# First softmax of taps ahead of the weights' loads, the last four tokens in twos, and a new order of steps

## The chip, the core and the metric

One NeuronCore of a Trainium2 chip runs the kernel. Its engines are TensorE (PE, with PEld for its weight loads), VectorE (DVE), ScalarE (ACT), GpSimd (POOL) and SyncE (SP, which issues DMAs); ACT issues a few DMAs too. The metric is the device time of one execution in microseconds (us); lower is better.

## The reference

`x` is 8 x 4160 x 192 and `weight_gen` 8 x 4160 x 8 x 7, both float32. Each token mixes itself and the six tokens before it, with seven taps per head; what comes out goes through a two-layer block of 192 -> 1024 -> 192.

```python
w = exp(weight_gen - max); w = w / (sum(w) + 1e-9)        # over the 7 taps of a head
x = einsum('bshk,bskhg->bshg', w, windows of x)           # causal, 8 heads of 24 columns
h = x @ w_in                                              # 1024 columns
solu = h * softmax(h)
ln = (solu - mean) / sqrt(var + 1e-6) * g_ln
out = ln @ w_out
```

## The kernel before

The 33,280 tokens lie on 128 partitions, 260 in a row on each, so a "token" below is one step of 128 rows; there are 260. They come in chunks of 4, 8, 8 and then 16 tokens (`starts` = 0, 4, 12, 20, 36, ...). For a chunk the kernel loads `xt` and `wt` and does the softmax of the taps in seven steps, t0 to t6: maximum on DVE (L112), subtraction on POOL (L114), exponential on ACT (L118), sum on DVE (L120), a copy on ACT (L122), reciprocal on DVE (L124), product on POOL (L126). ACT sums the squares of `xt` (L145).

POOL then does attention for a group of four tokens (two in the first four): a product over seven taps (L174) and two additions (L180, L182), which leave `half`. DVE adds its two parts into `a` (fin, L433). From there a token, or a pair, goes: a copy on ACT (dup, L439); transposition on PE (xT, L450); high part on ACT (xhi, L458); low part on DVE (xld, L479); first product on PE (mm1, L491 and L494); maximum on DVE (max, L505); exponential on ACT (exp, L509); product with it on DVE (solu, L515); squares on ACT (sq, L521); high half of the result on ACT (hi, L528); low half on DVE (lo, L532); a transposing DMA by SP (tr, L540); second product on PE (mm2, L580); scaling on ACT (out, L591); and for four tokens a store by SP (od, L594). The scales of a group of tokens are six short steps, f0 to f5, in turn on ACT (L555, L559/L561, L567) and DVE (L552). A first product writes `h` into one of three PSUM buffers, so that of token t waits for sq and lo of token t-3; second products share one buffer `po`, except for the odd two of the last four tokens, which take a buffer of `h`.

Before the first product the weights are converted: `w_in` in three parts (`raw_a` twice, and `raw_b`, shown as `hl`), `w_out` in four parts c0 to c3, each in three DVE instructions (L241, L244, L246), two on ACT (L248, L249) and three more on DVE (L253, L256, L260). Copies, remainders and norms follow (wa_hi, wa_lo, wb_hi, wb_lo, L284).

Each engine runs its own instructions in the order in which they were written. The order of the preparation stands in the code; that of all later steps comes from `issue_order`, a planner: it goes through a table of steps with an engine, an assumed cost, the steps waited for and sometimes an assumed earliest time (`ready`), and gives each free engine the able step with the lowest key, which is the token's number plus the step's number in `URGENCY`. `free` says when each engine is thought to come out of the preparation.

Of the kernel before, what the change touches and what calls it, by code (L numbers as in the profile page):

```python
# [26 lines left out]
def tile_kernel(ctx: ExitStack, tc: tile.TileContext, x, weight_gen, w_in, w_out, g_ln, out):  # L27
# [9 lines left out]
    RUN = B * S // P  # L37
    PB = P // B
    TG = 4
# [27 lines left out]
    def load_x(c, part=0):  # L67
        t0, n = starts[c], starts[c + 1] - starts[c]
        if part == 0:
            xs[c] = io.tile([P, (TC + HALO) * D], F32, name="xt")  # L70
        xt = xs[c]
        xv = xt.rearrange("p (t d) -> p t d", d=D)
        if c == 0:

            nc.gpsimd.memset(xt[:, : HALO * D], 0.0)
            nc.sync.dma_start(xv[:, HALO : HALO + n, :], x_run[:, :n, :])
            for b in range(B):
                queue = nc.sync if b % 2 else nc.scalar
                queue.dma_start(
                    xv[b * PB + 1 : (b + 1) * PB, :HALO, :],  # L80
                    x_run[b * PB : (b + 1) * PB - 1, RUN - HALO :, :],
                )
        elif t0 < HALO:
            first = xs[0].rearrange("p (t d) -> p t d", d=D)
            nc.sync.dma_start(xv[:, HALO : HALO + n, :], x_run[:, t0 : t0 + n, :])
            nc.sync.dma_start(xv[:, :HALO, :], first[:, t0 : t0 + HALO, :])
        else:
            cuts = [(HALO + n) * k // LOADS for k in range(LOADS + 1)]
            r0, r1 = cuts[part], cuts[part + 1]
            nc.sync.dma_start(xv[:, r0:r1, :], x_run[:, t0 - HALO + r0 : t0 - HALO + r1, :])  # L90
# [9 lines left out]
    TAP_STEPS = 7  # L100

    def softmax_taps(c, step):
        n = (starts[c + 1] - starts[c]) * H
        w3 = ws[c][:, : n * K].rearrange("p (n k) -> p n k", k=K)
        if step == 0:
            m = small.tile([P, TC * H], F32, name="wm", bufs=2)[:, :n]
            y = small.tile([P, TC * H], F32, name="wy", bufs=2)[:, :n]
            taps[c] = m, y
        m, y = taps[c]
        wide = [P, n, K]  # L110
        if step == 0:
            nc.vector.tensor_reduce(m, w3, axis=AX.X, op=ALU.max)  # L112
        elif step == 1:
            nc.gpsimd.tensor_tensor(  # L114
                out=w3, in0=w3, in1=m.unsqueeze(2).broadcast_to(wide), op=ALU.subtract
            )
        elif step == 2:
            nc.scalar.activation(w3, w3, AF.Exp)  # L118
        elif step == 3:
            nc.vector.tensor_reduce(m, w3, axis=AX.X, op=ALU.add)  # L120
        elif step == 4:
            nc.scalar.activation(y, m, AF.Copy, bias=1e-9)  # L122
        elif step == 5:
            nc.vector.reciprocal(y, y)  # L124
        elif step == 6:
            nc.gpsimd.tensor_tensor(  # L126
                out=w3, in0=w3, in1=y.unsqueeze(2).broadcast_to(wide), op=ALU.mult
            )
# [59 lines left out]
    w_in = w_in.bitcast(I32)  # L188
    w_out = w_out.bitcast(I32)
    load_x(0)  # L190
    raw_a = att.tile([P, 2 * FF], I32, name="raw_a", bufs=1)

    raw_b = big.tile([P, FF], I32, name="hl", bufs=3)
# [29 lines left out]
    column = const.tile([P, 1], F32, name="column")  # L223
    minus = const.tile([P, P], F32R, name="minus")
    nc.vector.tensor_scalar_mul(minus, ident, -1.0)

    for step in range(TAP_STEPS):
        softmax_taps(0, step)

    scratch = {}  # L230

# [173 lines left out]

    def stat_group(t):

        n = 2 if t < 2 * TG else TG
        return n if t % n == n - 1 else 0


    def group(t):

        if t < TG:
            return 2 if t % 2 == 0 else 0
        return TG if t % TG == 0 else 0

# [225 lines left out]


URGENCY = dict(
    a00=3.1, a01=2.3, a02=-28.9, a03=-6.5, a04=-3.6, a10=80, a11=-25.4, a12=-13, a13=-10, a14=10.4,
    attA=85.1, attB=2.4, b0=120.9, b1=-144.6, b2=138.3, b3=-1.5, b4=54.3, c00=-28.1, c01=85.1,
    c02=6.8, c10=-25.3, c11=31.3, c12=-72.7, c20=99.4, c21=-5.6, c22=10.2, c30=-149.7, c31=-14.5,
    c32=-100.3, dup=52.6, exp=-129.5, f0=8.2, f1=-120.4, f2=-71.5, f3=-118.4, f4=-66.1, f5=-45.6,
    fin=18.4, hi=-11, lo=33, lw=18.7, lx0=10.2, lx1=-115.4, lx2=-109.1, lx3=-20.7, max=-30,  # L650
    mm1=25.5, mm2=0.4, n0=-7.5, n1=11.8, n2=-1.8, n3=-113.6, n4=-8.6, n5=-69, n6=-123.6, od=-6.9,
    out=-81.2, p30=22.9, p31=0.5, p4=9.7, p5=12.6, p6=11.6, p70=-10.2, p71=-8.7, p80=20.3, p81=5.9,
    q00=7.1, q01=-5.1, q02=118.9, q10=-15.7, q11=20.7, q12=16.8, q20=100.6, q21=-95.2, q22=20.4,
    q30=143.8, q31=81.5, q32=98.3, solu=-7.6, sq=5, t0=5.1, t1=-3.7, t2=77.9, t3=44.1, t4=-26.5,
    t5=110.1, t6=267.2, tr=-13, v00=170.9, v01=5.1, v02=44, v03=0.2, v1=54.2, v2=58.8, v3=-12.2,
    v4=1, v5=21.2, xT=-66.9, xhi=-46.7, xld=30,
)


def issue_order(run, starts, group, stat_group, loads):  # L660
# [5 lines left out]

    PE, DVE, ACT, SP, POOL = range(5)
    SAME, CROSS = (25, 127, 143, 0, 102), 130
    free = [3000, 5900, 5000, 12000, 9050]
    steps, number = [], {}  # L670

    def add(name, t, engine, cost, *after, ready=0):
# [3 lines left out]
    def once(name, engine, cost, *after, ready=0):  # L676
        add(name, 0, engine, cost, *((x, 0) for x in after), ready=ready)
# [2 lines left out]
    parts = ["a0", "b", "a1", *(f"c{f}" for f in range(4))]  # L680
    for n, part in enumerate(parts):
        w_in, size = n < 3, 512 if n < 3 else 384
        at = (9000, 10500, 12000)[n] if w_in else 15000
        before = () if w_in else (f"{parts[n - 3]}4", "n" + {"a0": "0", "a1": "1", "b": "2"}[parts[n - 3]]) if n < 6 else ("q00",)
        if n:
            before += (parts[n - 1] + "0",)
        once(part + "0", DVE, 3 * (60 + size), *before, ready=at)
        once(part + "1", ACT, 2 * (190 + 0.85 * size), part + "0")
        once(part + "2", DVE, 3 * (60 + 1.04 * size), part + "1")
        if w_in:  # L690
            once(part + "3", ACT, 190 + 0.75 * size, part + "2")
            once(part + "4", DVE, 60 + 1.04 * size, part + "3")
            once("n" + {"a0": "0", "a1": "1", "b": "2"}[part], DVE, 60 + 1.04 * size, part + "2")
        else:
            f = n - 3
            once(f"q{f}0", ACT, 700, part + "2")
            once(f"q{f}1", PE, 660, f"q{f}0", *([f"q{f - 1}1"] if f else ["n6"]))
            once(f"q{f}2", ACT, 520, f"q{f}0")
    add("p30", 0, DVE, 868, ("q31", 0), ("mm1", 1))
# [31 lines left out]
        add("v4", t, DVE, 80, ("v3", t))  # L731
        add("v5", t, ACT, 240, ("v4", t))

    add("v00", 0, ACT, 1800, ready=9000)
    add_norms(0, 0)
    for c in range(1, len(starts) - 1):
        t, before = starts[c], starts[c - 1] if c > 1 else -1
        short = starts[c + 1] - t < 16
        if c > 1:
            add("lw", t, SP, 1270, last_group(c - 3))  # L740
            add("lx0", t, SP, 1540, last_group(c - 2), *parts_of(c - 2))
            for n in range(1, loads):
                add(f"lx{n}", t, SP, 1540, (f"lx{n - 1}", t))
        whole = starts[c + 1] - t == 16
        for part in range(4 if whole else 1):
            size = 830 if whole else 1800
            if c > 1:

                load = min(part + 1, loads - 1) if whole else loads - 1
                add(f"v0{part}", t, ACT, size, (f"lx{load}", t))  # L750
            else:
                add(f"v0{part}", t, ACT, size, ready=15000)
        add_norms(c, t)
        n = (starts[c + 1] - t) * 8
        on = (DVE, POOL, ACT, DVE, ACT, DVE, POOL)
        wide = 60 + 7.3 * n
        costs = (wide, 13.5 * n, 100 + 6 * n, wide, 100 + n, 60 + 6.3 * n, 13.5 * n)
        for k in range(7):
            if k:
                add(f"t{k}", t, on[k], costs[k], (f"t{k - 1}", t))  # L760
            elif c > 1:
                add("t0", t, on[k], costs[k], ("lw", t), ("t6", before))
            else:
                add("t0", t, on[k], costs[k], ready=12000)
# [4 lines left out]
    for i, t in enumerate(groups):  # L769
        c, full = chunk_of(t), group(t) == 4  # L770
        after = [("attB", groups[i - 1])] if i else []
        if c:
            after.append(("t6", starts[c]))
        if c > 1:
            after.append((f"lx{loads - 1}", starts[c]))
        add("attA", t, POOL, 14990 if full else 7500, *after, ready=15000 if c == 1 else 9000)
        add("attB", t, POOL, 3510 if full else 1800, ("attA", t), ("fin", groups[i - 2] if i > 1 else -1))
        old = t // 4 * 4 - 12
        add("dup", t, ACT, 307 if full else 200, ("fin", t))
        add("fin", t, DVE, 1710 if full else 880, ("attB", t), ("xT", old + 2 if old >= 0 else -1))  # L780
# [144 lines left out]
```

## Time and profile before

| | us |
|---|---|
| median of 3 runs (lowest, highest) | 1347.44 (1345.54, 1348.4) |
| profiled execution: its own time | 1347.67 |
| its span | 1345.8 |
| busy: PE, POOL, DVE, ACT | 1246.8, 1247.7, 1210.2, 1162.8 |

The span runs from the first to the last recorded instruction; 1.87 us of the profiled execution's time lie outside it. A row of the timeline reads: start, duration, engine, line, operation, out<-in and their shapes, and in brackets the idle time before it and what ended that. A row of a table of stretches gives the busy time of each engine in it, with the number of its instructions. "issue" is time in which an engine waited for nothing that the profile shows.

### The profile page before, as it was taken

What the parts mean: (1) busy time and instruction counts of PE and PEld (TensorE: products, weight loads), DVE (VectorE), ACT (ScalarE), POOL (GpSimd) and SP (SyncE); (2) the same over time, 40 slices, a digit from 0 to 9 for tenths busy, and PEclk for the clock granted to TensorE, in tenths of its full rate; (3) what the DMA queues carried; (4) which work ended last, traced back from release to release, by engine and by line L of the source; (5) the groups of instructions that cost most, each with busy time, mean ns of one, the idle gap of its engine ahead of it and who ended that gap; (6) DMA issues with size and microseconds to landing.
All of it is one profiled execution on the core that took longest, in us unless ns stands there. A gap on an engine that the chain in (4) does not pass through costs nothing.

```text
span 1345.8 us, 25810 instructions
## 1 busy us (share of the span) xinstructions
PE 1246.8 (93%) x9900; PEld 970.8 (72%) x9900; DVE 1210.2 (90%) x1588; ACT 1162.8 (86%) x2318; POOL 1247.7 (93%) x241
## 2 busy tenths in 40 slices
PE   0588899999999999999999999999999999999997
PEld 0365677777777777777777777777777777777776
DVE  5988899999999999999999999999999999889994
ACT  3778889889898988989898998989898898988886
POOL 5989899999999999999999999999999999999930
PEclk9899999999999999999999999999999999999999
DMA  5277668797886889688797968878787877976776
GB/s 180 74 159 169 139 134 201 123 207 137 155 179 134 196 137 208 125 179 163 129 202 140 191 140 180 162 128 203 140 193 137 183 150 138 183 134 123 133 134 130
DMA packets 565307, 210.31 MB, mean 156 GB/s; under 512 B 544456, under 2 KB 545864, under 8 KB 565184
## 3 DMA queue, kind: packets, MB, share of 16 engines
q1 hardware_dynamic: 563208, 206.55, 75.7%
q10 hardware_dynamic: 1976, 2.12, 0.6%
q8 instruction: 78, 1.28, 0.4%
q14 instruction: 45, 0.37, 0.1%
HBM read 46.15 MB, written 25.56 MB: 53 GB/s over the span
## 4 chain that ended last, share of the span: by engine, by line
ACT 43%; DVE 35%; issue 11%; PE 7%; DMA 2%; POOL 1%; SPq 0%; ACTq 0%; POOLq 0%
ACT hl L528 12%; ACT e L521 12%; DVE h L515 11%; DVE hl L532 11%; ACT e L509 9%; DVE stats L505 5%; DVE a L433 4%; ACT junk L145 3%; PE po L580 3%; PE h L494 2%; ACT x_hi L458 2%; ACT ot L591 2%; DMA hlT<-hl 2%; PE h L491 1%; DVE x_lo L479 1%
## 5 line engine op out<-in xcount | busy, mean ns | idle before, releaser
L174 POOL TENSOR_TENSOR pr<-xt,wt 128x5376 f32<-128x5376 f32 (+1 forms) x66 | 631.6, 9569 | 2.7
L580 PE MATMUL po<-w_hl,hlT 128*128 128x192 f16 x6192 | 555.1, 246 | 17.3 <-ACT ot L591 12.6
L580 PEld LDWEIGHTS <-hlT 128*128 128x128 f16 x6240 | 505.9, 98 | 83.2 <-issue 75.5
L515 DVE SCALAR_TENSOR_TENSOR h<-h,row,e 128x1024 f32<-128x1024 f32 x260 | 333.8, 1285 | 19.1 <-ACT e L509 16.9
L528 ACT ACTIVATE hl<-h 128x1024 f16<-128x1024 f32 x260 | 266.0, 1029 | 98.4 <-DVE h L515 55.4
L532 DVE SCALAR_TENSOR_TENSOR hl<-h,hl 128x1024 f16<-128x1024 f32 x260 | 316.5, 1218 | 36.8 <-ACT e L521 34.4
L180 POOL TENSOR_TENSOR pr<-pr 128x2304 f32<-128x2304 f32 (+1 forms) x66 | 333.0, 5045 | 5.2
L505 DVE TENSOR_REDUCE stats<-h 128x1 f32<-128x1024 f32 x260 | 316.3, 1217 | 3.9 <-PE h L494 3.3
L509 ACT ACTIVATE e<-h,stats 128x1024 f32<-128x1024 f32 x260 | 293.3, 1128 | 16.1 <-DVE stats L505 15.5
L521 ACT ACTIVATE e<-h,stats 128x1024 f32<-128x1024 f32 x260 | 293.0, 1127 | 1.1 <-DVE hl L532 1.0
L494 PE MATMUL h<-wa_hi,x_hi 128*128 128x512 f32 x520 | 234.0, 450 | 0.0
L182 POOL TENSOR_TENSOR half<-pr 128x1536 f32<-128x1536 f32 (+1 forms) x66 | 225.8, 3421 | 5.2
L494 PE MATMUL h<-wa_lo,x_hi 128*128 128x512 f32 x520 | 206.4, 397 | 0.0
L494 PE MATMUL h<-wa_hi,x_lo 128*128 128x512 f32 x520 | 205.9, 396 | 0.0
L494 PEld LDWEIGHTS h<-wa_hi,x_hi 128*128 128x128 f32 x520 | 98.1, 189 | 107.1 <-issue 95.5
L491 PE MATMUL h<-wb_hi,x_hi 64*128 64x512 f32 x520 | 131.0, 499 | 17.1 <-DVE hl L532 11.2
L433 DVE TENSOR_REDUCE a<-half 128x768 f32<-128x1536 f32 (+1 forms) x66 | 117.2, 1776 | 0.0
L591 ACT ACTIVATE ot<-po,stats 128x192 f32<-128x192 f32 x258 | 112.4, 436 | 3.6 <-PE po L580 3.6
L494 PEld LDWEIGHTS h<-wa_hi,x_lo 128*128 128x128 f32 x520 | 98.4, 189 | 23.2
L494 PEld LDWEIGHTS h<-wa_lo,x_hi 128*128 128x128 f32 x520 | 99.0, 190 | 12.0
L491 PE MATMUL h<-wb_hi,x_lo 64*128 64x512 f32 x520 | 104.2, 395 | 0.0
L450 PE MATMUL pa<-ident,a 128*128 128x128 f32 x520 | 81.2, 278 | 23.9 <-DVE x_lo L479 13.2
(89 smaller groups left out, 1072.0 us busy)
## 6 DMA issues: line engine op xcount, KB each, us to landing
out_dram<-ot SPq DMA_DIRECT2D x65, 384.0 KB, 3.3
xt<-in_x_dram SPq DMA_DIRECT2D x30, 576.0 KB, 4.8
xt<-in_x_dram SPq DMA_DIRECT2D x30, 480.0 KB, 4.4
wt<-in_weight_gen_dram SPq DMA_DIRECT2D x15, 448.0 KB, 4.8
hlT<-hl SPq DMA_TRANSPOSE x260, 4.7
xt<-in_x_dram SPq DMA_DIRECT2D x3, 384.0 KB, 4.6
raw_a<-in_moe_w_in_dram ACTq DMA_DIRECT2D x2, 512.0 KB, 7.4
raw<-in_moe_w_out_dram ACTq DMA_DIRECT2D x1, 768.0 KB, 12.2
```

Of the source, the lines that this page charges most:

```text
L174: nc.gpsimd.tensor_tensor(out=window(pr, 0, [(TG * D, K), (HG, n * H), (1, HG)]), in0=window(xt, t * D, [(D, K), (HG, n * H), (1, HG)]), i ...
L180: nc.gpsimd.tensor_tensor(out=pr[:, :3], in0=pr[:, :3], in1=pr[:, 3:6], op=ALU.add)
L182: nc.gpsimd.tensor_tensor(out=half, in0=window(pr, 0, [(2 * TG * D, 2), (D, n), (1, D)]), in1=window(pr, TG * D, [(5 * TG * D, 2), (D, n), ...
L491: nc.tensor.matmul(h[:, fs], lhs[rows, 1, :], rhs[rows], start=n == 0, stop=False)
L494: nc.tensor.matmul(h[:, fs], lhs[:, 0, :], rhs[:, fs], start=False, stop=n == 2)
L505: nc.vector.tensor_reduce(stat(t, NMAX), h_of[t], axis=AX.X, op=ALU.max, negate=True)
L509: nc.scalar.activation(e, h_of[t], AF.Exp, bias=stat(t, NMAX), accum_out=stat(t, Z))
L515: nc.vector.scalar_tensor_tensor(out=h, in0=h, scalar=row(t, SCALE), in1=e, op0=ALU.mult, op1=ALU.mult, accum_out=stat(t, M))
L521: nc.scalar.activation(e_of.pop(t), h_of[t], AF.Square, bias=stat(t, M), scale=-float(FF), accum_out=stat(t, Q),)
L528: nc.scalar.activation(hl[:, 0, :], h_of[t], AF.Copy, scale=2.0**14)
L532: nc.vector.scalar_tensor_tensor(out=hl[:, 1, :], in0=h_of[t], scalar=2.0**14, in1=hl[:, 0, :], op0=ALU.mult, op1=ALU.subtract,)
L580: nc.tensor.matmul(po[:, :D], hlT[:, half * NJ + j, :], w2_hl[:, j, w, :], start=n == 0, stop=n == len(terms) - 1,)
```

## The change

It has three parts. The seven softmax steps of the first chunk are written right after the loads of its `wt` and `xt`, ahead of the loads of the weights. The last four tokens go through attention in two groups of two (`group`), and their scales are computed in two groups of two (`stat_group`). And the order is made anew: all 100 numbers of `URGENCY`, three numbers of `free` and several `ready` times are others, and `q{f}0`, which scales a part of `w_out`, now waits for two steps of the conversion of `w_in` too.

```diff
     load_x(0)
+    for step in range(TAP_STEPS):
+        softmax_taps(0, step)
     raw_a = att.tile([P, 2 * FF], I32, name="raw_a", bufs=1)
...
     nc.vector.tensor_scalar_mul(minus, ident, -1.0)
-
-    for step in range(TAP_STEPS):
-        softmax_taps(0, step)
...
     def stat_group(t):
-        n = 2 if t < 2 * TG else TG
+        n = 2 if t < 2 * TG or t >= RUN - TG else TG
...
     def group(t):
-        if t < TG:
+        if t < TG or t >= RUN - TG:
             return 2 if t % 2 == 0 else 0
...
-    a00=3.1, a01=2.3, a02=-28.9, a03=-6.5, a04=-3.6, a10=80, a11=-25.4, a12=-13, a13=-10, a14=10.4,
+    a00=116.4, a01=5.1, a02=-29.3, a03=20.5, a04=44.5, a10=8.5, a11=-82.2, a12=-38.6, a13=-3.9,
...
-    free = [3000, 5900, 5000, 12000, 9050]
+    free = [3000, 5600, 7700, 12000, 6200]
...
-        at = (9000, 10500, 12000)[n] if w_in else 15000
+        at = (12000, 12000, 12500)[n] if w_in else 20000
...
-            once(f"q{f}0", ACT, 700, part + "2")
+            once(f"q{f}0", ACT, 700, part + "2", "a02", "a12")
...
-    add("v00", 0, ACT, 1800, ready=9000)
+    add("v00", 0, ACT, 1800, ready=10000)
...
-                add(f"v0{part}", t, ACT, size, ready=15000)
+                add(f"v0{part}", t, ACT, size, ready=21500)
...
-        add("attA", t, POOL, 14990 if full else 7500, *after, ready=15000 if c == 1 else 9000)
+        add("attA", t, POOL, 14990 if full else 7500, *after, ready=21500 if c == 1 else 10000)
```

The changed kernel is one line shorter, so most lines of the program stand one number lower there.

What this does to the order shows at three places. The first is DVE at the start. `wm` and `wy` are the taps' maxima, sums and reciprocals, 32 columns for the first chunk and 64 for the second; `minus` is a constant; `h<-raw_a` and `h<-hl` are the conversion of `w_in`. Before:

```order
L112 TENSOR_REDUCE wm<-wt 128x32
L225 TENSOR_SCALAR minus<-ident 128x128
L241 TENSOR_SCALAR h<-raw_a 128x512
L244 TENSOR_SCALAR h<-raw_a 128x512
L246 TENSOR_SCALAR h<-h 128x512
L241 TENSOR_SCALAR h<-hl 128x512
L244 TENSOR_SCALAR h<-hl 128x512
L120 TENSOR_REDUCE wm<-wt 128x32
L246 TENSOR_SCALAR h<-h 128x512
L124 RECIPROCAL wy<-wy 128x32
```

And DVE at the same place now:

```order
L112 TENSOR_REDUCE wm<-wt 128x32
L227 TENSOR_SCALAR minus<-ident 128x128
L120 TENSOR_REDUCE wm<-wt 128x32
L124 RECIPROCAL wy<-wy 128x32
L151 TENSOR_REDUCE row<-squares_x 128x1
L112 TENSOR_REDUCE wm<-wt 128x64
L240 TENSOR_SCALAR h<-raw_a 128x512
L243 TENSOR_SCALAR h<-raw_a 128x512
L245 TENSOR_SCALAR h<-h 128x512
L240 TENSOR_SCALAR h<-hl 128x512
```

The sum and the reciprocal of the first chunk's taps moved ahead of the conversion, and so did a sum of squares and the maximum of the second chunk's taps, which before stood eleven rows behind the first instruction of the conversion.

The second place is ACT at the start; `raw_101` (now `raw_110`) is `w_out`, and `junk,squares_x<-xt` the squares of the first chunk. Before:

```order
L79 DMA xt<-in_x_dram 15x1152 x4
L195 DMA raw_a<-in_moe_w_in_dram 128x1024 x2
L202 DMA raw_101<-in_moe_w_out_dram 128x4x384
L206 DMA g<-in_moe_g_ln_dram 128x8x1
L118 ACTIVATE wt<-wt 128x224
L145 ACTIVATE junk,squares_x<-xt 128x1920
L122 ACTIVATE wy<-wm 128x32
```

And ACT there now:

```order
L79 DMA xt<-in_x_dram 15x1152 x4
L197 DMA raw_a<-in_moe_w_in_dram 128x1024
L118 ACTIVATE wt<-wt 128x224
L197 DMA raw_a<-in_moe_w_in_dram 128x1024
L122 ACTIVATE wy<-wm 128x32
L204 DMA raw_110<-in_moe_w_out_dram 128x4x384
L208 DMA g<-in_moe_g_ln_dram 128x8x1
L145 ACTIVATE junk,squares_x<-xt 128x1920
```

The exponential stands behind one load of `w_in` in place of all four loads, and the copy of the sums behind two.

The third place is ACT at the end, from hi of token 258 on. `hl<-h` is hi, `e,stats<-h,stats` is exp in line L509 (now L508) and sq in line L521 (now L520), `ot<-po` is out, and the rest are scales. Before:

```order
L528 ACTIVATE hl<-h 128x1024
L521 ACTIVATE e,stats<-h,stats 128x1024
L509 ACTIVATE e,stats<-h,stats 128x1024
L591 ACTIVATE ot<-po,stats 128x192
L555 ACTIVATE stats<-stats,row 128x4
L528 ACTIVATE hl<-h 128x1024
L521 ACTIVATE e,stats<-h,stats 128x1024
L591 ACTIVATE ot<-po,stats 128x192
L559 ACTIVATE stats<-stats 128x4
```

And ACT there now:

```order
L527 ACTIVATE hl<-h 128x1024
L558 ACTIVATE stats<-stats 128x2
L560 ACTIVATE stats<-stats 128x2x2
L508 ACTIVATE e,stats<-h,stats 128x1024
L590 ACTIVATE ot<-po,stats 128x192
L566 ACTIVATE stats<-stats,newton 128x2
L554 ACTIVATE stats<-stats,row 128x2
L520 ACTIVATE e,stats<-h,stats 128x1024
L527 ACTIVATE hl<-h 128x1024
L590 ACTIVATE ot<-po,stats 128x192
L520 ACTIVATE e,stats<-h,stats 128x1024
```

The exponential of the last token moved ahead of the squares of the token before it, and these, with two short steps of the scales, now stand between it and the last hi. On PE the first products of tokens 8 and 9, of 11 and 12 and of 14 and 15 stood in reversed turn before and stand in turn now (2 and 3, and 5 and 6, are reversed in both); and at the end the first product of token 259 is followed by seven second products where six followed before.

More of the change, by code (lines that the diff above doesn't have):

```diff
@@ L645 @@
 URGENCY = dict(
-    a00=3.1, a01=2.3, a02=-28.9, a03=-6.5, a04=-3.6, a10=80, a11=-25.4, a12=-13, a13=-10, a14=10.4,
[L647 to L656, printed above, removed]
+    a00=116.4, a01=5.1, a02=-29.3, a03=20.5, a04=44.5, a10=8.5, a11=-82.2, a12=-38.6, a13=-3.9,
+    a14=119, attA=-124.6, attB=-25.1, b0=-6.2, b1=122.2, b2=-9.4, b3=-11.3, b4=34, c00=14,
+    c01=15.4, c02=18.2, c10=-68.8, c11=-13.3, c12=3, c20=55.1, c21=-29.3, c22=-115.7, c30=-94.3,
+    c31=-1.8, c32=-140.4, dup=-95.8, exp=-34.3, f0=-18.5, f1=-39.2, f2=-126.7, f3=-51.5, f4=-125.9,
+    f5=-152.9, fin=4.4, hi=-109.4, lo=-131.8, lw=91.4, lx0=-85.3, lx1=2.6, lx2=19.1, lx3=-46.7,
+    max=3.4, mm1=175.8, mm2=76.4, n0=173.6, n1=7.4, n2=57.2, n3=3, n4=-27.1, n5=-84.1, n6=99.5,
+    od=-14.7, out=-199.8, p30=127.1, p31=28.9, p4=8.8, p5=109.2, p6=119.6, p70=-71, p71=24.7,
+    p80=-32.1, p81=-12.3, q00=6, q01=-5.2, q02=-87.2, q10=-174.6, q11=-23.4, q12=61.7, q20=-8,
+    q21=-53.6, q22=-0.5, q30=30.4, q31=88, q32=-5.3, solu=-60.1, sq=32.6, t0=26, t1=90.9, t2=3.3,
+    t3=130.7, t4=60.7, t5=7.5, t6=-108.4, tr=-25.1, v00=33.9, v01=14, v02=104.7, v03=1.6, v1=11.8,
+    v2=64.1, v3=-8.3, v4=-13.2, v5=124.2, xT=-2, xhi=4.1, xld=2.3,
 )
```

## The prediction

> **What bounds the kernel now.** I read the table of stretches first, then the waits of POOL and PE, then the timelines of the start and of the end. Three stretches: an early one, a chunk of 16 tokens from the middle, and 16 late tokens, when no taps are left to be prepared. The columns are time, then busy PE, PEld, DVE, ACT and POOL.
>
> ```profile
> 100.00:200.00 100.00, 88.97 (x686) 68.03 (x684) 89.06 (x115) 86.46 (x174) 92.17 (x19) 0.98 0.72 147
> 615.70:693.55 77.85, 75.88 (x610) 59.15 (x608) 72.29 (x93) 69.88 (x140) 76.65 (x16) 1.00 0.81 163
> 1180.00:1255.70 75.70, 75.16 (x606) 59.39 (x604) 68.55 (x90) 66.00 (x128) 74.76 (x13) 1.00 0.68 130
> ```
>
> In the middle PE lacks 1.97 us of a chunk's 77.85 and POOL 1.2: two engines are full at once. Without the work for taps 16 tokens take 75.7. Which of the two leads is told by who waits. The first two rows are POOL's waits in the whole run, the others PE's waits in one middle chunk (total, times, longest):
>
> ```profile
> POOL wt L126 <- DVE wy L124: 13.7, 2, 13.3
> POOL wt L126 <- DVE stats L552: 3.9, 9, 0.5
> ...
> PE pa L450 <- DVE x_lo L479: 0.5, 1, 0.5
> PE h L491 <- ACT e L521: 0.5, 1, 0.5
> PE h L491 <- DVE hl L532: 0.5, 1, 0.5
> PE po L580 <- ACT ot L591: 0.4, 1, 0.4
> ```
>
> In the middle POOL waits 0.43 us at a time for the reciprocal of the taps, which DVE reaches in its own order, that is, at PE's pace; PE waits half a microsecond here and there for DVE and ACT. So PE with its two helpers sets the pace, with POOL 0.4 us of 77.85 behind. An earlier POOL alone shortens the middle by 0.43 a chunk at most.
>
> The early stretch is worse than either. 42 rows of this kind, two for each of 21 tokens, reach from 45.8 to 164.0:
>
> ```profile
> L491 PE MATMUL h<-wb_hi,x_hi x42: 467/497/792, 45.8 to 164.0; 64*128 64x512 f32 x42
> ...
>   DVE hl L532: 9.1, 6
> ```
>
> 20 tokens in 118.2 us, where the middle's pace (77.85/16 = 4.87) gives 97.3: 20.9 us are lost, 9.1 of them in six waits for lo.
>
> **The start.** Waits of the first chunk's softmax behind other work:
>
> ```profile
> 3.25 0.58 POOL L114 TENSOR_TENSOR wt<-wt,wm 128x224 f32<-128x224 f32 x1 [0.94 <-DVE wm L112]
> 6.06 0.37 ACTq L195 DMA_DIRECT2D raw_a<-in_moe_w_in_dram  x1
> 8.86 0.39 ACT L118 ACTIVATE wt<-wt 128x224 f32<-128x224 f32 x1 [6.84 <-issue]
> 12.38 0.69 DVE L241 TENSOR_SCALAR h<-raw_a 128x512 int32<-128x512 int32 x1 [9.09 <-DMA raw_a<-in_moe_w_in_dram]
> 15.77 0.38 DVE L120 TENSOR_REDUCE wm<-wt 128x32 f32<-128x224 f32 x1
> 16.66 0.34 DVE L124 RECIPROCAL wy<-wy 128x32 f32<-128x32 f32 x1
> 17.08 0.58 POOL L126 TENSOR_TENSOR wt<-wt,wy 128x224 f32<-128x224 f32 x1 [13.26 <-DVE wy L124]
> 17.73 4.95 POOL L174 TENSOR_TENSOR pr<-xt,wt 128x2688 f32<-128x2688 f32 x1
> 25.46 1.81 POOL L182 TENSOR_TENSOR half<-pr 128x768 f32<-128x768 f32 x1
> 38.12 0.97 POOL L126 TENSOR_TENSOR wt<-wt,wy 128x448 f32<-128x448 f32 x1 [0.42 <-DVE wy L124]
> 39.17 9.71 POOL L174 TENSOR_TENSOR pr<-xt,wt 128x5376 f32<-128x5376 f32 x1
> ```
>
> POOL has subtracted at 3.83; the exponential waits in ACT's queue behind the loads until 8.86, the sum in DVE's behind L241, which waits for `raw_a`. Now only the first load of `raw_a` (6.06 + 0.37) stands ahead: exponential to 6.85, sum to 7.3, copy (about 0.25) to 7.6, reciprocal to 8.0, product to 8.7. The second load of `raw_a` goes out about 0.3 later, half of `w_out` and `g` about 0.6 later. Nothing needs those two for 10 us; the second `raw_a` is converted third. First attention: 8.7 for 17.73, 9 us earlier, if `xt` is there (ACT used it at 9.15 without a wait; at worst that, and a few tenths less gained).
>
> But POOL's next product of taps comes after two groups of two at 9.54 each and a subtraction: at 8.7 + 20 = 28.7 it wants the reciprocal of the second chunk, and that stands in DVE's order behind the maximum of the same chunk, now ahead of the conversion, and 28 rows more. When does that chunk's `wt` land? Its issue, the landing of the two loads of `wt` issued up to 15 us (minimum, median, maximum: 2.0 is the first, 8.6 the second), and the maximum where it stood:
>
> ```profile
> 6.94 0.56 SPq L96 DMA_DIRECT2D wt<-in_weight_gen_dram  x1
> DMA to landing us min/median/max: 2.0/5.3/8.6
> 19.60 0.61 DVE L112 TENSOR_REDUCE wm<-wt 128x64 f32<-128x448 f32 x1
> ```
>
> 6.94 + 8.6 = 15.5. Before, nobody waited for it, since DVE came at 19.60. Now DVE waits, with the whole conversion queued behind: L112 ends at 16.1, and the conversion starts there and not at 12.38. This is a wait that the change adds. The 28 rows to L124, nearly all on 512 columns, at the 0.69 of L241: 19.3, so the reciprocal starts at 35.4, and POOL goes on at 36.0 for 38.12. Of the 9 us 2 are left at once. (If `wt` were there at 12.38, 5 would be.)
>
> The rule that speaks against this wait is in the Trainium skill, DMA: Bandwidth & Descriptors, section "Queues, rings and completion order": each DMA engine goes round-robin between the queues that have work, packet by packet. By it SP's queue (512 KB of `w_in` and 224 KB of `wt`) would be through when as much of ACT's has moved; the trace's landing of 8.6 does not agree, so I keep 15.5 and make the equal share a rival.
>
> **The early stretch.** Where POOL and PE then lose time:
>
> ```profile
> 80.01 1.08 DVE L112 TENSOR_REDUCE wm<-wt 128x128 f32<-128x896 f32 x1
> 81.17 1.75 POOL L114 TENSOR_TENSOR wt<-wt,wm 128x896 f32<-128x896 f32 x1 [3.37 <-DVE wm L112]
> 150.48 1.76 POOL L114 TENSOR_TENSOR wt<-wt,wm 128x896 f32<-128x896 f32 x1 [6.33 <-DVE row L151]
> 128.52 0.80 PE L491 MATMUL h<-wb_hi,x_hi 64*128 64x512 f32 x2 [2.44 <-DVE hl L532]
> 129.12 0.63 PE L491 MATMUL h<-wb_lo,x_hi 64*128 64x512 f32 x2
> 149.38 0.40 PE L491 MATMUL h<-wb_lo,x_hi 64*128 64x512 f32 x2
> ```
>
> POOL stands 9.7 us for maxima that DVE reaches late. DVE gets to the first of the two at about the same place in its order now, so POOL, 2 us earlier there, may just wait longer; the second subtraction comes one group later in POOL's order, with more time for DVE. PE pays twice for a wait: after 2.44 us of it a matmul takes 0.63 in place of 0.40. In the order of before the first products of tokens 8 and 9, 11 and 12, 14 and 15 are exchanged on PE; now they go in turn from token 7 on, which should spare waits for lo. I cannot price a whole order from rows. The ends are: a gain of nothing, as DVE starts the conversion 3.7 us later, and of 12, if all six waits for lo go with their slow matmuls (9.1, and six times about half a microsecond). I take the middle, -6: the order that made these waits is gone, but it was not these alone that POOL and DVE stood for.
>
> **The middle.** The work is the same, and the order differs. From 164 to 1290 are 14.5 chunks. Below there is POOL's wait of 0.43 (14.5 x 0.43 = 6.2 us to gain); above there is no floor. What stands in the same place in both orders: taps are ready about 30 tokens ahead, attention runs some 7 tokens ahead of PE, transpositions one or two products ahead. Second products run six tokens behind where five did, a little more slack. I take -0.5.
>
> **The end.**
>
> ```profile
> 1286.95 3.48 POOL L182 TENSOR_TENSOR half<-pr 128x1536 f32<-128x1536 f32 x1
> 1325.90 1.23 DVE L505 TENSOR_REDUCE stats<-h 128x1 f32<-128x1024 f32 x1
> 1326.71 1.11 ACT L521 ACTIVATE e<-h,stats 128x1024 f32<-128x1024 f32 x1
> 1327.80 1.11 ACT L509 ACTIVATE e<-h,stats 128x1024 f32<-128x1024 f32 x1
> 1330.46 1.02 ACT L528 ACTIVATE hl<-h 128x1024 f16<-128x1024 f32 x1 [0.86 <-DVE h L515]
> 1332.69 1.23 DVE L532 SCALAR_TENSOR_TENSOR hl<-h,hl 128x1024 f16<-128x1024 f32 x1
> 1333.98 1.78 SPq L540 DMA_TRANSPOSE hlT<-hl  x1
> 1339.94 2.15 PE L580 MATMUL h<-w_hl,hlT 128*128 128x192 f16 x24 [0.90 <-DMA hlT<-hl]
> 1342.58 0.34 SPq L594 DMA_DIRECT2D out_dram<-ot  x1
> ```
>
> POOL is done 55 us before the end; PE has a backlog, so the groups of two give nothing, and cost nothing: 2 x 9.54 for 18.55 on POOL is covered by that backlog, and the extra short steps on DVE and ACT by engines that lack 7 to 10 us of 75.7. In the last chain exp (free at 1327.13) waited 0.7 behind sq, and lo (free at 1331.5) 1.2 behind the last sq. Both now go first; but sq of token 258, out and two scales stand between exp and the last hi, about 2.3 us where solu takes 1.4: 0.9 lost. One more second product goes behind the last first product: up to 2.15 earlier, less what six second products in a row wait for `po`. Ends 0 and -3; I take -1.5.
>
> **Sum.** 1347.67 (the profiled execution, 0.23 above the median) -6 -0.5 -1.5 = 1339.7, or 1339.5 against the median.
>
> **Rivals.** Within 0.2% (2.7 us) is about what a measurement of this kernel can't tell from no change.
> - Equal shares of the queues: `wt` lands near 12.8 and the conversion starts 2.7 us sooner: 1337. For it speaks only that the load is small; the row of its landing speaks against it. 7%.
> - All waits of the early stretch go and the middle is held by POOL alone: -12 -5 -3 gives 1327.5. For it: the waits are of order, not of work. 12%.
> - The first attention is earlier and nothing follows: POOL stands at the second chunk's taps, DVE at `wt`, PE starts when it did; the middle is PE's. Only the end is left: 1346. 13%.
> - Slower: the new order makes PE wait more in each chunk. Place: the first product of token t behind sq and lo of token t-3, since hi goes ahead of sq more often now. One microsecond a chunk costs 14.5 and gives 1354; it decides from 0.55 a chunk on (8/14.5). The waits of 0.5 show that the slack there is used up; against it, the order within a token is nearly the same. 13%.
>
> The forecast keeps 55%. Faster: 55 + 7 + 12 = 74%; same 13%; slower 13%. The range, 1328 to 1350, leaves out the fourth rival and half of the second.
>
> **What would show it.** First attention near 8.7; DVE's L112 on 64 columns ending at 16 after a wait for `wt`; POOL's second product of taps at 36; the 21st token's first product near 158 where it was at 164.0; a chunk in the middle at 77.4 to 77.9; some 54 us from POOL's last instruction to the end. A chunk of 78.5 or more would make the prediction wrong, whatever the start does.

## The result: 1.5% slower, and the profile after

The changed kernel takes 1368.07 us (median of 4 runs, 1366.43 to 1368.75), the kernel before 1347.88 in the same session: a ratio of 1.0151, 95% interval 1.0134 to 1.0169. The profiled execution of after has a span of 1364.6 us, 18.8 more than before. The forecast was 1339.5.

Where the 18.8 us are is told by cutting the span at two first products (L490 now, L491 before): the 25th token's (number 24), which starts at 183.06 us before and at 174.67 after, and the 257th's (number 256), at 1309.86 and 1327.97. Up to the first cut after is 8.4 us ahead, between the cuts it loses 26.5, and from the second cut to the span's end it takes 36.6 for 35.9. The stretch between the cuts and the one behind them, before and then after (time, then busy PE, PEld, DVE, ACT, POOL; the figure behind the five is the granted TensorE clock):

```profile
183.06:1309.86 1126.80, 1100.90 (x8818) 858.59 (x8818) 1040.93 (x1339) 1006.46 (x1991) 1091.86 (x197) 1.00 0.80 159
1309.86:1345.84 35.98, 28.39 (x265) 23.73 (x264) 19.06 (x27) 22.53 (x45) 0.00 (x0) 1.00 0.60 128
174.67:1327.97 1153.30, 1107.21 (x8817) 864.21 (x8817) 1046.89 (x1345) 1008.75 (x1996) 1090.45 (x202) 0.99 0.76 156
1327.97:1364.64 36.67, 30.35 (x289) 25.77 (x288) 18.96 (x29) 22.94 (x50) 0.00 (x0) 1.00 0.58 120
```

The last stretch holds 24 matmuls more after than before, which is one second product: at each cut the new order has done one less. So some 2 us of PE's work (30.35 us for 28.39) only move from the start to the end. Without that the start gained about 6.4 us, and the end about 1.3, which is what PE has less of idle time there (6.3 us for 7.6).

Of the 26.5 us 20.2 are idle time of PE (46.1 for 25.9) and 6.3 are longer matmuls. The loss comes mostly in one chunk of two. After, two neighbouring stretches of 16 first products:

```profile
622.38:698.80 76.42, 73.97 (x584) 57.19 (x584) 71.08 (x93) 69.26 (x139) 72.18 (x14) 1.00 0.80 167
698.80:782.24 83.44, 78.07 (x632) 61.59 (x632) 73.91 (x96) 72.28 (x142) 80.50 (x16) 1.00 0.73 152
```

The second holds two second products more than the first (632 matmuls for 584; 610 in the 77.85 us of before), which is some 4 of the 7 us between them. The rest is idle time of PE: 2.4 us in the first and 5.4 in the second, for 2.0 before. In such a slow stretch one group of four takes 23 to 25 us where its neighbours take 19.

From the list of waits between 180 and 1300 us (total, times, longest) these are ACT's for a DMA, POOL's largest and those of PE's matmuls for other engines; after:

```profile
ACT junk L145 <- DMA xt<-in_x_dram: 36.5, 15, 4.0
POOL wt L126 <- DVE wy L124: 22.2, 4, 13.4
PE po L579 <- ACT ot L590: 21.2, 21, 2.0
PE h L490 <- ACT e L520: 10.2, 14, 1.2
PE pa L449 <- ACT a L438: 6.4, 2, 3.2
PE pa L449 <- DVE x_lo L478: 3.7, 7, 1.8
PE h L490 <- DVE hl L531: 2.9, 5, 1.1
```

The same of before, where POOL's largest is the 3.9 that the prediction shows:

```profile
PE pa L450 <- DVE x_lo L479: 8.2, 17, 0.5
PE h L491 <- DVE hl L532: 6.0, 13, 0.5
PE h L491 <- ACT e L521: 5.9, 12, 0.5
PE po L580 <- ACT ot L591: 4.1, 11, 0.4
ACT junk L145 <- DMA xt<-in_x_dram: 1.5, 1, 1.5
PE pa L450 <- ACT a L439: 0.7, 2, 0.5
```

ACT stood 36.5 us at L145, the squares of the next chunk's `xt`, for 1.5 before. One of these waits, on four engines (SP's loads; ACT; DVE; PE):

```profile
279.83 3.37 SPq L539 DMA_TRANSPOSE hlT<-hl  x1
283.25 0.57 SPq L90 DMA_DIRECT2D xt<-in_x_dram  x1
...
284.93 0.21 ACT L520 ACTIVATION_READ_ACCUMULATOR e<-h,stats 128x1 f32 x1
288.11 0.84 ACT L145 ACTIVATE junk<-xt 128x768 f32<-128x768 f32 x1 [2.97 <-DMA xt<-in_x_dram]
288.95 0.39 ACT L438 COPY a<-a 128x256 f32<-128x256 f32 x1
289.24 1.01 ACT L527 ACTIVATE hl<-h 128x1024 f16<-128x1024 f32 x1
...
283.60 1.78 DVE L432 TENSOR_REDUCE a<-half 128x768 f32<-128x1536 f32 x1
290.29 1.22 DVE L531 SCALAR_TENSOR_TENSOR hl<-h,hl 128x1024 f16<-128x1024 f32 x1 [1.58 <-ACT hl L527]
...
289.39 0.87 PE L449 MATMUL pa<-ident,a 128*128 128x128 f32 x3 [3.21 <-ACT a L438]
290.19 0.79 PE L490 MATMUL h<-wb_hi,x_hi 64*128 64x512 f32 x2
290.78 0.63 PE L490 MATMUL h<-wb_lo,x_hi 64*128 64x512 f32 x2
296.61 0.40 PE L490 MATMUL h<-wb_lo,x_hi 64*128 64x512 f32 x2
```

ACT was free at 285.14. Its next instruction is a square, and the load of x that it needs had gone out at 283.25, behind a transposition on SP; it was there 4.86 us later. Behind the square stands the copy (dup, L438), whose input DVE had finished at 285.4. It could have run at once; ACT keeps its order, so it ran at 288.95, and PE, which waits for it to transpose, stood 3.21 us. Then PE paid again: 0.63 us a matmul in place of 0.40. The granted clock says why (a stretch right after the wait, and the next):

```profile
289.40:292.80 3.40, 3.40 (x12) 2.12 (x13) 2.33 (x2) 2.74 (x5) 3.40 (x1) 0.51 1.08 268
293.10:297.00 3.90, 3.90 (x38) 3.19 (x36) 2.67 (x3) 3.88 (x8) 3.90 (x2) 1.00 0.82 216
```

How long such a load takes stands on the page of after (KB each, median us from issue to landing); the page of before had 4.8 and 4.4:

```profile
xt<-in_x_dram SPq DMA_DIRECT2D x30, 576.0 KB, 4.8
xt<-in_x_dram SPq DMA_DIRECT2D x30, 480.0 KB, 4.3
```

So a square needs four to five us between the issue of its load and ACT's turn. ACT has 97 steps in a chunk of 77.85 us, one in 0.8 us on average. Counted in the two orders, the ACT steps between a load of x and its square (first, second, third, fourth square of a chunk), for four of the chunks:

```
chunk at token   68             100            132            180
before           8 10 12 11     8 10 12 11     8 10 12 11     8 10 12 11
after            5  5 19  5     7  9 23 10     7  9 23 10     5  5 19  5
```

In these chunks of before no square has fewer than 8; in after six have 5. (The single wait of before, 1.5 us, is at a square of the last chunk, which has 4.) But the count does not decide alone: the longest wait, 4.04 us, is at the first square of the chunk at token 132, which has seven steps. Its load and the square:

```profile
608.02 0.42 SPq L90 DMA_DIRECT2D xt<-in_x_dram  x1
612.80 0.84 ACT L145 ACTIVATE junk<-xt 128x768 f32<-128x768 f32 x1 [4.04 <-DMA xt<-in_x_dram]
```

SP sent the load late, behind a transposition and a store, and ACT was free for the square 0.75 us after the issue. What divides the cases is this time, from the issue to ACT's turn, read from the timelines of SP and ACT. In the chunks at tokens 52 to 228 of before it is 5.3 to 7.9 us, and no square there waits for its load. In after it is 0.75 to 3.7 us at all 15 squares that wait, and 4.06 or more at all others from token 52 on, which wait 0.14 at most.

### The profile page after: what moved, and what is told of

It is laid out like the page before. It is cut to its first block, busy times and chain, and to the rows that moved or that the text cites. A ratio compares the mean times of both kernels' runs of the same rounds, so it can differ in the third digit from the quotient of the medians.

```text
span 1364.6 us, 25861 instructions
## 1 busy us (share of the span) xinstructions
PE 1254.2 (92%) x9900; PEld 976.5 (72%) x9900; DVE 1212.0 (89%) x1592; ACT 1161.7 (85%) x2323; POOL 1248.1 (91%) x244
## 4 chain that ended last, share of the span: by engine, by line
PE 31%; ACT 29%; DVE 22%; issue 10%; DMA 6%; SPq 1%; ACTq 0%; DVEq 0%
PE po L579 12%; PE h L493 11%; ACT e L508 8%; ACT hl L527 7%; ACT e L520 7%; DVE h L514 7%; PE h L490 6%; DVE hl L531 5%; DMA xt<-in_x_dram 5%; DVE a L432 3%; DVE stats L504 3%; ACT ot L590 2%; PE pa L449 2%; ACT junk L145 1%; ACT x_hi L457 1%
## 5 line engine op out<-in xcount | busy, mean ns | idle before, releaser
L579 PE MATMUL po<-w_hl,hlT 128*128 128x192 f16 x6192 | 557.3, 247 | 28.8 <-ACT ot L590 26.7
L520 ACT ACTIVATE e<-h,stats 128x1024 f32<-128x1024 f32 x260 | 290.9, 1119 | 8.2 <-DVE hl L531 7.9
L508 ACT ACTIVATE e<-h,stats 128x1024 f32<-128x1024 f32 x260 | 292.1, 1124 | 6.3 <-DVE stats L551 2.9
L490 PE MATMUL h<-wb_hi,x_hi 64*128 64x512 f32 x520 | 131.2, 501 | 17.7 <-ACT e L520 12.5
L449 PE MATMUL pa<-ident,a 128*128 128x128 f32 x520 | 84.1, 282 | 50.3 <-DVE a L432 36.1
L449 PEld LDWEIGHTS pa<-ident,a 128*128 128x128 f32 x520 | 61.1, 143 | 66.2 <-DVE a L432 27.1
```

Source lines behind the costliest of these rows:

```text
L490: nc.tensor.matmul(h[:, fs], lhs[rows, 1, :], rhs[rows], start=n == 0, stop=False)
L508: nc.scalar.activation(e, h_of[t], AF.Exp, bias=stat(t, NMAX), accum_out=stat(t, Z))
L520: nc.scalar.activation(e_of.pop(t), h_of[t], AF.Square, bias=stat(t, M), scale=-float(FF), accum_out=stat(t, Q),)
L579: nc.tensor.matmul(po[:, :D], hlT[:, half * NJ + j, :], w2_hl[:, j, w, :], start=n == 0, stop=n == len(terms) - 1,)
```

## Experiments: which part, and which mechanism

The theory after this reading: the loss is in the new order alone, and in it at one place, ACT's squares ahead of the landing of x. The rivals: taps first or the twos carry it; or the rest of the new order on ACT (hi ahead of sq and lo, out, the scales) makes PE wait, and the squares stand where ACT had time anyway.

**The parts apart.** The first run takes taps first and the twos out of the changed kernel, the second puts them into the kernel before; neither touches the numbers of the order it has. The second, as a diff to before:

```diff
     load_x(0)
+    for step in range(TAP_STEPS):
+        softmax_taps(0, step)
...
-    for step in range(TAP_STEPS):
-        softmax_taps(0, step)
...
-        n = 2 if t < 2 * TG else TG
+        n = 2 if t < 2 * TG or t >= RUN - TG else TG
...
-        if t < TG:
+        if t < TG or t >= RUN - TG:
```

> The changed kernel with the softmax of the first taps issued where it was before, and the last four tokens as one group of four again; the order made anew is kept. Theory (the loss of 26.5 us between the 25th token and the last four is in the new order alone): the middle stays 25 to 28 us longer than before, and the time is 1366 to 1378 us, since the 8 us gained at the start shrink too. Rival (taps first or the twos cause the middle's loss, for instance because POOL runs further ahead): the middle is back within 5 us of before, 1340 to 1355 us.

> The kernel before with the other two parts of the change alone: the first taps issued ahead of the loads of the weights, and the last four tokens and their scales in twos; the numbers that set the order are those of before. Theory (the loss is in the order): no loss in the middle (within 2 us of before), L145's waits for x at most 8 us in all, 1342 to 1349 us. Rival (the two parts carry the loss): 1355 us or more.

The new order alone took 1371.17 us, ratio 1.0172 (1.0157 to 1.0187), with a middle of 1155.6 us between the same cuts, 28.8 longer than before where 25 to 28 were expected. The two other parts alone took 1344.72, ratio 0.9977 (0.9967 to 0.9987), with a middle of 1126.4. The loss is in the order.

**The squares later, the squares sooner.** `spaced` goes through the finished order and moves a square until the given number of ACT steps lies between its load and it; all else stays in its place.

```diff
-    for op, t in issue_order(RUN, starts, group, stat_group, LOADS):
+    plan = issue_order(RUN, starts, group, stat_group, LOADS)
+    for op, t in spaced(plan, dict(v00=12, v01=12, v03=12)):    # changed kernel
+    for op, t in spaced(plan, dict(v00=5, v01=5, v03=5)):       # kernel before
```

> The changed kernel with one kind of instruction moved on one engine: from the chunk at token 52 on, the squares v00, v01 and v03 stand 12 ACT steps behind the load that they wait for, where 5 to 10 steps were (before had 8 to 12). Theory (ACT stands at a square whose x has not landed, and all behind it waits, PE with it): the 36.5 us of L145's waits between 160 and 1300 us fall under 8, the groups of four that took 23 to 25 us take 19 to 21, and the time falls by 15 to 26 us, to 1342 to 1353. Rival (the squares only stand where ACT had time; the rest of the new order, hi ahead of sq and lo, out and the scales, makes PE wait): the waits of L145 fall just the same, PE waits elsewhere, and the time falls by less than 5 us, 1363 to 1368.

> The kernel before with the counterpart: from the chunk at token 52 on, the squares v00, v01 and v03 stand 5 ACT steps behind the load that they wait for, where 8 to 11 steps were; all else as before. Theory (squares ahead of their landing hold ACT): L145's waits rise from 1.5 us to 30 us or more between 180 and 1300 us, and the time rises by 10 to 25 us, to 1358 to 1373. Rival (they wait in time that ACT has to spare): L145's waits rise, the time stays within 3 us of before.

Later: 1345.16 us, ratio 0.9978 (0.9968 to 0.9987), 22.9 us less than the changed kernel; no wait of L145 is left in the list between 180 and 1300 us; but the slowest group of four still takes 23.4, where 19 to 21 were expected. Sooner: 1384.71 us, ratio 1.0269 (1.0249 to 1.0289), 36.7 more than before. From the waits of the second:

```profile
POOL wt L126 <- DVE stats L552: 39.8, 12, 5.7
PE po L580 <- ACT ot L591: 29.5, 26, 2.4
ACT junk L145 <- DMA xt<-in_x_dram: 21.3, 20, 2.2
```

In the direction both came out as the theory said. In size the second did not: the waits rose to 21.3 us, not to 30, and the time by more than the range allowed. POOL's line is a likely reason: in the order of before POOL is only 0.4 us a chunk from being the bound, and now it waits 39.8 us (3.9 before) for the reciprocal of the taps, which DVE reaches later when ACT holds it up.

**The loads sooner, ACT untouched.** Moving squares also changes what ACT does when. So the other end was moved: the second to fourth load of a chunk's x go ahead of the transposition right before them on SP, and the orders of the four other engines stay row for row.

```diff
+    for name, t in [x for x in order if x[0] in ("lx1", "lx2", "lx3") and x[1] >= 52]:
+        i = order.index((name, t))
+        j = max(n for n in range(i) if order[n][0] == "tr")
+        order.insert(j, order.pop(i))
```

> The changed kernel with rows moved on SP alone: from the chunk at token 52 on, the second, third and fourth load of x each go out ahead of the transposition (tr) that stood right before them; ACT, DVE, PE and POOL keep their orders. Theory (ACT stands at squares whose x has not landed): the loads land 3 to 5 us earlier, L145's waits fall from 36.5 us to under 12, the time falls by 12 to 24 us, to 1344 to 1356. Rival (the run with the squares later got its 23 us from another arrangement on ACT, not from the landing): the waits fall, the time falls by less than 5 us, 1363 or more. A cost that could take from the gain: a transposition lands later behind the load.

1337.54 us, ratio 0.9920 (0.9903 to 0.9936): 30.5 us less than the changed kernel where 12 to 24 were expected, and faster than before. L145's waits fall from 36.5 to 4.0 us and PE's for `po` from 21.2 to 9.5; POOL's for the taps go too:

```profile
PE po L579 <- ACT ot L590: 9.5, 7, 1.6
PE h L490 <- ACT e L520: 7.7, 12, 1.0
POOL wt L126 <- DVE wy L124: 4.1, 3, 2.2
ACT junk L145 <- DMA xt<-in_x_dram: 4.0, 5, 1.5
```

The stretch between the two cuts is 1122.66 us now, 4.1 shorter than before:

```profile
175.83:1298.49 1122.66, 1098.76 (x8817) 859.66 (x8816) 1045.50 (x1345) 1009.20 (x1996) 1088.99 (x201) 1.00 0.78 160
```

The same instructions of ACT, DVE, PE and POOL in the same order: the loss was the landing, not the arrangement. This run gained 7.6 us more than the one with the squares later; there POOL still waits 9.0 us for the taps (4.1 here), and the slowest group of four takes 23.4 us (22.6 here). Where the 7.6 us come from was not tried. In that slowest group ACT has two or three squares and two tap steps more than in its neighbours; that this is the cause of what remains is likely, and was not tried.

**Controls.** The same move in the kernel before, which had one such wait; and more of the same in the changed kernel, all loads of a chunk back to back:

> The kernel before with the same move on SP: from the chunk at token 52 on, the second, third and fourth load of x each ahead of the transposition that stood right before them. Theory (the move is worth what ACT stood waiting for x, and before stood 1.5 us for it between 180 and 1300 us): within 3 us of before, 1345 to 1350 us. Rival (loads ahead help for another reason, for instance the transpositions or POOL's attention come sooner): 1330 to 1342 us.

> The changed kernel with all four loads of x of a chunk issued one right behind the other (from the chunk at token 52 on), where one transposition stood between each two. Theory: L145 waits for nothing (it had 4.0 us left with the loads one place ahead), and a second product has six tokens of slack for its transposition: within 3 us of the run with loads one place ahead, 1335 to 1341 us. Rival (the transposition queued behind 2.1 MB of x lands later than PE needs it, or ACT's waits return elsewhere): 1342 us or more, with PE waiting for hlT.

The control took 1345.78 us, ratio 0.9982 (0.9973 to 0.9991): 1.9 us less, about the 1.5 that ACT had stood. The move is worth about what it takes from ACT's wait, here and in the changed kernel (30.5 us for 32.5 of waits).

All loads together took 1350.47 us, ratio 1.0016 (1.0005 to 1.0026): 12.9 worse than one place ahead, as the rival's time said, but by neither mechanism it named. L145 waits for nothing, and PE's weight loads wait 0.3 us for `hlT`. DVE now does what ACT did, and PE's matmuls wait 13.4 us for DVE's x_lo, for 2.3 with the loads one place ahead. In the list of waits from 180 to 1300 us:

```profile
DVE wm L112 <- DMA wt<-in_weight_gen_dram: 17.8, 7, 4.7
```

The load of the next chunk's `wt` had stood between the first load of x and the second; now it stands behind all four. One instance, in the timelines of SP, DVE and PE:

```profile
435.79 2.41 SPq L90 DMA_DIRECT2D xt<-in_x_dram  x4
438.25 0.57 SPq L96 DMA_DIRECT2D wt<-in_weight_gen_dram  x1
...
447.13 1.09 DVE L112 TENSOR_REDUCE wm<-wt 128x128 f32<-128x896 f32 x1 [4.73 <-DMA wt<-in_weight_gen_dram]
...
451.20 0.66 PE L449 MATMUL pa<-ident,a 128*128 128x128 f32 x4 [3.47 <-DVE x_lo L478]
```

DVE's maximum started 8.9 us after the issue of `wt`, and PE then stood 3.47 us for DVE's x_lo.

**Taps first, and the twos.** What is each worth once the order is sound?

> The kernel before with the first taps issued ahead of the weights' loads alone; the order and the last four tokens are those of before. Theory (taps first is worth 3 to 5 us at the start, and the twos at the end cost 1.7, which the run with both showed from the last group's first product to the end, 34.8 us for 33.1): 1341.5 to 1344 us. Rival (the twos cost nothing): as with both, 1344 to 1346.

> The new order without the two other parts (first taps where they were, last four tokens as one group), with the loads of x one place ahead on SP. Theory (the new order is good but for the squares ahead of their landing, and taps first is worth 3 us beside it, as the order alone with 1371.2 for 1368.1 showed): 1339 to 1342 us, faster than before. Rival (the new order only gains with taps first, since it was made for it): 1345 us or more.

> The changed kernel with the loads of x one place ahead, and the last four tokens as one group of four. Theory (the twos cost and give nothing that can be measured: in the order of before 1344.7 with and 1345.5 without, in the joined order 1347.2 and 1347.3): within 1.5 us of 1337.5. Rival (the twos are worth the 1.5 us of the prediction): 1338.5 to 1340.5.

Taps first alone on before: 1345.53 us, ratio 0.9981 (0.9969 to 0.9994); with the twos it was 1344.72, so the twos did not cost the 1.7 us that I expected. The order alone with loads ahead: 1338.67, ratio 0.9931 (0.9917 to 0.9946). Loads ahead without the twos: 1336.19, ratio 0.9914 (0.9901 to 0.9928), the fastest of all. With twos and without differ by 1.4 us, and in the order of before by 0.8 the other way: nothing that these runs separate. Of the 10.7 us that the version with loads ahead gains on before, 9.0 are there without taps first and twos.

That taps first gives little in the order of before has a reason in the trace of the run with taps first and twos: the first attention starts at 14.11 us there, not at 8.81. The sum is done by 7.5, but the reciprocal stands in DVE's order behind the first conversion, which waits for `raw_a`:

```profile
12.43 0.69 DVE L241 TENSOR_SCALAR h<-raw_a 128x512 int32<-128x512 int32 x1 [4.91 <-DMA raw_a<-in_moe_w_in_dram]
13.03 0.34 DVE L124 RECIPROCAL wy<-wy 128x32 f32<-128x32 f32 x1
```

**A join that failed.** All steps up to the 25th token's first product in the new order, all later ones in the order of before, to have the better start with the middle of before:

> The changed kernel (taps first, twos) with two orders joined: all steps that the order of before has up to the first product of token 24 go in the new order, all later ones in the order of before. Theory (the new order gains at the start and loses only in the middle): the 25th token's first product at 174 to 177 us as with the new order, a middle of 1126 to 1128 us as before, an end of 35: 1337 to 1341 us. Rival (POOL is no earlier with the new order, 35.5 us for 36.2 at the third attention, and in the order of before POOL is only 0.4 us a chunk behind PE, so PE's lead at the start is waited off in the middle): the middle takes 1130 or more, 1342 to 1346 us.

> The same as the joined order, with the last four tokens as one group of four. Theory (the twos cost 1.7 us at the end): 1 to 2.5 us less than the joined order with twos. Rival (they cost nothing): within 0.5 us of it.

1347.18 us, ratio 0.9989 (0.9979 to 0.9999), and 1347.31, ratio 0.9994 (0.9985 to 1.0003). The first is slower than theory and rival had it; the second shows again no cost of the twos. The first product of token 24 is at 178.2 and 177.7 us, 5 ahead of before, and the four tokens right behind the join take 24.7 us in both (19.5 before); from there on a group of four takes what it took before. So the lead is lost at the seam, not waited off over the middle as the rival had it. Which engine is out of step there was not looked into.

## Why the prediction was wrong

- **The start: right.** Forecast: first attention at 8.7 us, DVE's maximum on 64 columns waiting for `wt` and done at 16.1, POOL's second product of taps at 36.0. In the changed kernel:

```profile
8.81 4.94 POOL L174 TENSOR_TENSOR pr<-xt,wt 128x2688 f32<-128x2688 f32 x1
15.31 0.62 DVE L112 TENSOR_REDUCE wm<-wt 128x64 f32<-128x448 f32 x1 [4.57 <-DMA wt<-in_weight_gen_dram]
34.43 0.97 POOL L126 TENSOR_TENSOR wt<-wt,wy 128x448 f32<-128x448 f32 x1 [5.68 <-DVE wy L124]
```

  The wait that the change adds is there, with the landing taken from before; the rival of equal shares (12.8, for which the text shows no sum) is out. POOL went on 1.6 us earlier than forecast.
- **The early stretch: right in sign and nearly in size, the size in part by luck.** 20 tokens in 111.16 us for 118.20, 7.0 for the 6 forecast, of which some 2 are the second product that the new order puts off. The 6 was the middle between 0 and 12, not a sum of waits; the 21st first product at 155.86, forecast 158. The waits for lo went (9.1 us to 0.2), and 5.8 us of waits for sq took part of their place.
- **The middle: wrong, -0.5 against +26.5.** This is the step that failed. The text compared four things in the two orders (taps, attention, transpositions, second products) and found them in nearly the same places. It did not compare the squares of x with the loads they wait for, the one step on ACT in the middle whose input comes straight from a DMA. The page of before had the landing, 4.8 us, and its list of waits a single one of 1.5 us at L145: a slack that was just enough, in most chunks 5.3 us or more from the issue to ACT's turn. The new order took it away at 15 squares, where 0.75 to 3.7 us are left: ACT stands 36.5 us there, and PE behind it. The sign that the text gave for being wrong, a chunk of 78.5 us or more, came: 79.5 on average (1153.30 / 14.5).
- **The fourth rival: right side, wrong place.** Held at 13%, it priced a microsecond a chunk at 14.5 and gave 1354. Measured is 1.83 a chunk (26.5 / 14.5). But it put the wait at the first product behind sq and lo. Those two waits of PE in the middle are 13.1 us after and 11.9 before; what grew is PE's wait for ACT's out (17 us more) and for its copy (5.7 more). With the loads ahead these two waits fall from 21.2 and 6.4 us to 9.5 and 0.9.
- **The end: about right, though the cut hides it.** -1.5 forecast; 36.6 us for 35.9 from the last cut, with one second product more in it: PE is idle 1.3 us less. The last second product no longer waits for its transposition (0.90 us before). POOL's last instruction ends 61.6 us ahead of the end, not 54, since PE lost time in the middle. The pairs of runs with and without twos show nothing either way.
- **The sum.** -8.4 + 26.5 + 0.7 = 18.8, or -6.4 + 26.5 - 1.3 with the second product that moved put back. With the loads ahead, which changes the failed step alone, the time is 1337.54, 2 us under the forecast; there the new order's middle is 4.1 us shorter than before, more than the 0.5 that I had allowed it.

## What to carry to other kernels

Where an order of instructions is made anew, look first at those that wait for a DMA directly on an engine that others wait for: set the time from the issue of the load to the engine's turn for its user against the landing in the profile. A count of the instructions between them is only a first hint, since the load itself may go out late. Here one square that came early held ACT 2.97 us, TensorE stood 3.21 for it, and its clock fell as well. Giving three such loads one place more on their queue was worth 30 us; sending all four loads back to back lost 13 of them again, since the load behind them then came late for another engine.

## What the runs showed of the hardware

The Trainium skill says (PSUM — Partial Sum Buffer, section "Engine vs sequencer instructions") that the queues of ScalarE, VectorE and GpSimdE are strict FIFO. The trace agrees on ACT: the copy with its input ready at 285.4 us ran at 288.95, behind the square.

TensorE's clock fell after short waits: 0.51 granted in the 3.4 us after a wait of 3.21 us (full again by 293.1), and in the kernel before 0.63 us a matmul after one of 2.44. The length of the wait alone does not tell: in the changed kernel the clock fell after one of 1.84 us (0.71 from 373.4 to 376.8) and stayed at 1.00 after one of 1.97 (615.0 to 617.2). In the middle of the changed kernel matmuls are slow at three places, from 289, 375 and 850 us on, and in that of before at none. With as many matmuls in both middles, PE's 6.3 us more of busy time are put down to this; they are part of the 26.5 lost. The Trainium skill's page TensorE: Matmul & The Clock Gate (section "What's actually happening") gives an idle window of about 3.4 us for the fall to half rate. Here less was enough.
